# Sliding-window attention and a cosine-gated MLP on one core: where four matmuls of tile 0 stand, and how batch 0's shifted rows of v are made

## The chip, the core and the metric

One core of a Trainium2 chip runs the whole program. Its engines work side by side, each through its own list of instructions in order: TensorE (PE in the profile; PEld is its weight load), VectorE (DVE), ScalarE (ACT), GpSimd (POOL) and SyncE (SP). They wait for one another by semaphores. Transfers run on 16 DMA engines that all queues share: q0 is filled by GpSimd, q1 by SyncE. TensorE writes to PSUM, of which this kernel names eight banks: O0, O1, S, X0, X1 and three called t.

The metric is the device time in microseconds, the median of several executions. Before the change it is 306.59 us (306.25 to 306.64 in three runs).

## The reference

```python
# q, k, v: (8 batches, 8 heads, 576 rows, 64); w_in: (512, 2048); w_out: (2048, 512)
scores = scale * q @ k^T                      # scale = 1 / sqrt(64)
mask = (rel >= 0) & (rel < 64)                # rel = row of q - row of k
attn = exp(scores - max) / (sum + 1e-9)
x = (attn @ v)                                # (4608, 512): a row for each token, heads side by side
h = x @ w_in
out = (h * cos(h)) @ w_out                    # float32
```

## The kernel before

The 4608 rows are cut into nine tiles of 512 (MT); a batch has 576 rows, so a tile takes its rows from one or two batches. Rows are handled in blocks of 64: block j of a batch sees only the columns of blocks j - 1 and j. Two heads make a pair, and there are four pairs; `xT[mt]` holds a tile's x transposed, 128 rows of a pair by 512 columns.

For attention the names are: `tq`, `tk` (transpose q and k of a pair), `pq`, `pk` (copy them out of PSUM), `s` (scores of four blocks), `m` (negated maximum), `e` (exponential, ScalarE), `i` (reciprocal of the sum, VectorE), `n` (product with it, on GpSimd with `.p` or VectorE with `.d`), `w` (transpose the weights), `c` (copy that out of PSUM), `v` (weights times v, into `o_ps`) and `x` (copy `o_ps` into `xT`, on ScalarE with `.a` or VectorE with `.d`). The first number behind a name is the pair, the second the half of its blocks.

For the MLP, tile by tile: `first(mt, ff, ks, ...)` (line 348) is one matmul of 128 x 512: slice `ff` of h (16 of them) gets the part of pair `ks`. Four of them finish a slice; ScalarE takes its sine (cos as a shifted sine, line 513), VectorE multiplies (line 516), and 64 matmuls of line 528 make the tile's output.

Tile 0 and batch 0 have no work of an earlier tile to lie beside. Their order is written out by hand as a list of steps, FIRST (line 41), that one loop walks (line 482); it fixes the order on all engines. After it a planner (`at`, `pump`) puts the work of later batches between the slices of the current tile, by due times counted in slices.

In tile 0 the first three slices of h (SKEW = 3) start early: the step `h.p` does the matmuls of slices 0 to 2 for pair p as soon as x of that pair is there. Slices 3 to 15 follow, four matmuls each, once x is complete. Each slice takes the bank that H_FIRST lists: O1, X0, X1, S, O0, and again. The same banks have held the scores (S_FIRST).

The weights are multiplied with v in windows of 128 rows. An even window starts at a multiple of 128 and is loaded straight into slot 0, 2, 4 or 6 of `vtiles` (`load_v`, by GpSimd's DMAs). An odd slot is shifted by 64 rows and put together within SBUF: its partitions 0 to 63 are the even slot behind it, its partitions 64 to 127 the even slot ahead of it (`spread_v`, line 166). For batch 0 the step `z.1.p` is GpSimd's copy of the upper halves of slots 1, 3, 5 and 7, and `z.0.d` VectorE's copy of the lower halves of 1, 3 and 5. Batch 1's are made by two DMAs of SyncE, later ones by VectorE.

`l` in FIRST issues the next of the large loads, on GpSimd's queue: three parts of w_in, q and k of batch 1, two halves of w_out. `tb` loads ScalarE's sine table.

Of the kernel before, what the change touches and what calls it, by code (L numbers as in the profile page):

```python
# [10 lines left out]
def _safe_warn(msg, *a, **kw):  # L11
# [20 lines left out]
PAIRS = 4  # L32
# [3 lines left out]
SKEW = 3  # L36
# [4 lines left out]
FIRST = (  # L41
# [6 lines left out]
)  # L48


# [1 line left out]
def kernel(  # L52
# [9 lines left out]
    nc = tc.nc  # L62
# [18 lines left out]
    vtiles = [const.tile([128, NU - 1, d_model], BF16, name=f"v{i}") for i in range(3)]  # L81
# [21 lines left out]
    def bank(which, name):  # L103
        if which == "t":
            return ps_t.tile([128, 512], F32, tag="t", name=name)
        return ps.tile([128, 512], F32, tag=which, name=name)

    def copy(engine, out, in_):
        {"a": nc.scalar.copy, "p": nc.gpsimd.tensor_copy}.get(engine, nc.vector.tensor_copy)(out, in_)  # L109
# [46 lines left out]
    def values_of(b):  # L156
        return rowtiles[0][:, 0:8 * d_model].rearrange("p (s x) -> p s x", s=8) if b == B - 1 else vtiles[b % 3]

    def load_v(b, c):
        n = 128 if c < 4 else 64  # L160
        vt = values_of(b)[:n, 2 * c if c < 4 else 2 * c - 1]
        nc.gpsimd.dma_start(out=vt.rearrange("p (h d) -> p h d", h=H),  # L162
                            in_=v[b, :, c * 128:c * 128 + n, :].rearrange("h p d -> p h d"))


    def spread_v(b, half, engine="p"):
        vt = values_of(b)
        to, of = ((vt[0:64, 1:7:2], vt[0:64, 2:8:2]), (vt[64:128, 1:8:2], vt[64:128, 0:7:2]))[half]
        if engine == "dma":
            nc.sync.dma_start(out=to, in_=of)  # L170
        else:
            copy(engine, to, of)
# [18 lines left out]
    def put(name, b, p, engine=None):  # L191
        of = st.pop(("t" + name, b, p)).rearrange("d (c p) -> d p c", c=RC)
        to = halves(turned(b))[name][:, p].rearrange("d (p c) -> d p c", c=RC)
        if b or name == "k":
            copy(engine, to, of)
        elif engine == "a":
            nc.scalar.mul(to, of, scale)
        else:
            nc.vector.tensor_scalar(to, of, scale, None, ALU.mult)
# [33 lines left out]
    def g_scores(n, which):  # L233
        s_ps = bank(S_FIRST[which], "s_ps")
        units = groups[n]
        s_ps = s_ps[:, 0:len(units) * 128].rearrange("p (u c) -> p u c", c=128)
        m0 = 2 if units[0][2] else 0
        nc.tensor.matmul(out=s_ps.rearrange("p u c -> p (u c)"), lhsT=ident,
                         rhs=mask16[:, m0:m0 + len(units)].rearrange("p u c -> p (u c)"),
                         start=True, stop=False, skip_group_check=True)  # L240
        for u, (b, p, j) in enumerate(units):
            for h in range(2):
                d = slice(64 * h, 64 * h + 64)
                nc.tensor.matmul(out=s_ps[d, u].rearrange("p (a t) -> p a t", a=2), lhsT=q_cols(b, p, j)[d],
                                 rhs=k_cols(b, p, j)[d], start=False, stop=u == len(units) - 1, skip_group_check=True)
        st["s", n] = s_ps
        st.update({("cross", unit): 0 for unit in units})
# [100 lines left out]
    def first(mt, ff, ks, start, stop):  # L348
        if start:
            st["h", ff] = bank((H_FIRST, H_SECOND, H_BANKS)[min(mt, 2)][ff], "h_ps")  # L350
        nc.tensor.matmul(out=st["h", ff], lhsT=w_in_sb[:, ks, ff * 128:ff * 128 + 128],  # L351
                         rhs=st["xT", mt][:, ks], start=start, stop=stop)

    def skew(mt):
        return 5 if mt == 1 else SKEW

    def skewed(mt, ks, n):
        for ff in range(skew(mt)):
            first(mt, ff, ks, n == 0, n == PAIRS - 1)

    def last_rows(gT, o_sb):
# [19 lines left out]
    def pump(time):  # L381
        plan.sort(key=lambda x: x[:2])
        while plan and plan[0][0] <= time:
            _, _, fn, args = plan.pop(0)
            fn(*args)
# [3 lines left out]
    n = n_first  # L389
# [71 lines left out]
            load_heads(name, 0, p0, n)  # L461
    for c in range(4):
        load_v(0, c)
    loads = iter([(load_w_in, 0, 512), (load_w_in, 512, 1280), (load_w_in, 1280, 2048),
                  (load_heads, "q", 1), (load_heads, "k", 1), (load_w_out, 0, 8), (load_w_out, 8, 16)])

    def load():
# [3 lines left out]
    turn_s, turn_h = iter(range(100)), iter(range(100))  # L471
    steps = {"tq": lambda p: transposed("q", 0, (p,)), "tk": lambda p: transposed("k", 0, (p,)),
             "pq": lambda p, engine=None: put("q", 0, p, engine),
             "pk": lambda p, engine="a": put("k", 0, p, engine),
             "mk": put_masks, "l": load, "tb": sine_table, "h": lambda p: skewed(0, p, next(turn_h)),
             "z": lambda half, engine=None: spread_v(0, half, engine),
             "s": lambda p, g: g_scores(2 * p + g, next(turn_s) % 5), "m": lambda p, g: g_max(2 * p + g),
             "e": lambda p, g: g_exp(2 * p + g), "i": lambda p, g: g_inv(2 * p + g),
             "n": lambda p, g, engine: g_norm(2 * p + g, engine), "w": lambda p, g: g_trans(2 * p + g),
# [9 lines left out]
    for mt in range(n_mt):  # L489
        base = mt * T  # L490
        gT = []
        if mt:
            for ks in range(PAIRS):
                pump(max([base - 1] + [time for time, _, fn, args in plan
                                       if fn is put_x and args[:2] == (mt, ks)
                                       or mt == 1 and fn is values and args == (mt, ks + 1)]))
                if mt > 1 or ks < 2:
                    skewed(mt, ks, ks)
            if mt == 1:
                for ff in range(skew(1)):  # L500
                    for ks in range(2, PAIRS):
                        first(1, ff, ks, False, ks == PAIRS - 1)
        for ff in range(n_ff):
            for ks in range(PAIRS):
                if ff >= skew(mt):
                    first(mt, ff, ks, ks == 0, ks == PAIRS - 1)
            h_ps = st.pop(("h", ff))
            sin = moe.tile([128, MT], F32, tag="sin", name="sin", bufs=4)
            if ff % 2 == 0:
                gt = moe.tile([128, 2, MT], BF16, tag="gT", name="gT", bufs=n_ff // 2 + 2)  # L510
                gT.append(gt)
            e = ff % 2
            nc.scalar.activation(sin, h_ps, AF.Sin, bias=math.pi / 2.0)  # L513
            if ff == n_ff - 1 and mt < B - 1:
                exp_table()
            nc.vector.tensor_tensor(out=gt[:, e], in0=h_ps, in1=sin, op=ALU.mult)  # L516
            pump(base + ff)
        half = n_ff // 2 if mt == 0 else n_ff
        for ms0 in range(0, MT // 128, 2):
            o_sb = moe.tile([128, 2, d_model], F32, tag="out", name="out_sb", bufs=3)  # L520
            o_ps = [bank(which, "out_ps") for which in (("O0",) if mt == n_mt - 1 and ms0 else ("O0", "O1"))]
            for step, (lo, e) in enumerate([(lo, e) for lo in range(0, n_ff, half) for e in range(2)]):
                ms = ms0 + e
                if mt == n_mt - 1 and ms == MT // 128 - 1:
                    last_rows(gT, o_sb)
                    break
                for ff in range(lo, lo + half):
                    nc.tensor.matmul(out=o_ps[e], lhsT=gT[ff // 2][:, ff % 2, ms * 128:ms * 128 + 128],  # L528
                                     rhs=w_out_sb[:, ff], start=ff == 0, stop=ff == n_ff - 1)
                    if ff % 4 == 3:  # L530
                        if ff == n_ff - 1:
                            if mt or not ms0 or e:
                                copy("a" if e else "d", o_sb[:, e], o_ps[e])
                            else:
                                at(Q + 13.97, copy, "d", o_sb[:, e], o_ps[e])
                            if mt == n_mt - 1:
                                store(o_sb, mt, ms0, e, 1)
                        pump(base + Q + 4 * ms0 + step * half // 4 + ff % half // 4)
            if mt < n_mt - 1:
                at(base + T + (1.5 if mt else 3) + ms0 / 2, store, o_sb, mt, ms0, 0, 2)  # L540
# [30 lines left out]
```

## Time and profile before

| | |
|---|---|
| median of three runs | 306.59 us |
| profiled execution | 306.21 us |
| its span, first to last instruction | 304.3 us |
| TensorE busy (PE) | 291.6 us, 96% |
| ScalarE busy | 235.8 us, 77% |
| VectorE busy | 218.5 us, 72% |
| GpSimd busy | 171.1 us, 56% |
| granted TensorE clock | 1.00 in all stages |
| h's matmuls (L351) | 576, 127.3 us busy |
| output's matmuls (L528) | 560, 125.1 us busy |

Instructions are shown as engine, line, operation and output<-input. A row of a timeline has the start and the duration in us, the number of instructions merged (x3), and in brackets how long the engine was idle before and what ended that. "Busy" overstates TensorE a little, since its matmuls are pipelined and their ends modelled. Lines such as L109 are those of a helper that many steps call, so such a row is told by the names of its tiles. An engine's idle time costs something only where others wait for that engine.

### The profile page before, as it was taken

What the parts mean: (1) busy time and instruction counts of PE and PEld (TensorE: products, weight loads), DVE (VectorE), ACT (ScalarE), POOL (GpSimd) and SP (SyncE); (2) the same over time, 40 slices, a digit from 0 to 9 for tenths busy, and PEclk for the clock granted to TensorE, in tenths of its full rate; (3) what the DMA queues carried; (4) which work ended last, traced back from release to release, by engine and by line L of the source; (5) the groups of instructions that cost most, each with busy time, mean ns of one, the idle gap of its engine ahead of it and who ended that gap; (6) DMA issues with size and microseconds to landing.
All of it is one profiled execution on the core that took longest, in us unless ns stands there. A gap on an engine that the chain in (4) does not pass through costs nothing.

```text
span 304.3 us, 7887 instructions
## 1 busy us (share of the span) xinstructions
PE 291.6 (96%) x2668; PEld 141.7 (47%) x2668; DVE 218.5 (72%) x833; ACT 235.8 (77%) x787; POOL 171.1 (56%) x198
## 2 busy tenths in 40 slices
PE   2968999999999999999999999999999999999996
PEld 1744444544454445444544444444444454454443
DVE  2896889688787878787877787778788877236701
ACT  4798699967997799779987998799869986106600
POOL 8996156967774976497659765967533630000000
PEclk9999999999999999999999999999999999999999
DMA  8999999699979998999999999999993441011012
GB/s 155 175 211 207 208 159 136 100 162 178 230 132 153 220 165 138 148 196 190 143 159 204 185 121 173 151 220 126 185 171 107 87 132 61 0 72 70 0 69 71
DMA packets 165577, 43.88 MB, mean 144 GB/s; under 512 B 154720, under 2 KB 160800, under 8 KB 165536
## 3 DMA queue, kind: packets, MB, share of 16 engines
q0 software_dynamic: 99344, 18.06, 75.6%
q1 hardware_dynamic: 66048, 25.11, 40.7%
q8 instruction: 21, 0.34, 0.4%
q10 hardware_dynamic: 144, 0.20, 0.2%
q14 instruction: 20, 0.16, 0.2%
HBM read 36.70 MB, written 9.44 MB: 152 GB/s over the span
## 4 chain that ended last, share of the span: by engine, by line
PE 87%; ACT 6%; DVE 3%; DMA 1%; issue 1%; POOL 0%; SPq 0%; DVEq 0%; POOLq 0%; ACTq 0%
PE h_ps L351 41%; PE out_ps L528 37%; ACT e L288 4%; PE o_ps L330 3%; PE s_ps L261 3%; PE out_ps L366 1%; DMA first_f<-in_k_dram 1%; DVE s L277 1%; PE tq_ps L186 1%; ACT wT L109 0%; DVE w L302 0%; PE tk_ps L186 0%; DVE out_sb L109 0%; ACT L343 0%; ACT L346 0%
## 5 line engine op out<-in xcount | busy, mean ns | idle before, releaser
L351 PE MATMUL h_ps<-xT,w_in 128*128 128x512 bf16 x576 | 127.3, 379 | 1.3 <-DVE xT L109 0.6
L528 PE MATMUL out_ps<-w_out,gT 128*128 128x512 bf16 x560 | 125.1, 380 | 0.2 <-DVE gT L516 0.2
L516 DVE TENSOR_TENSOR gT<-h_ps,sin 128x512 bf16<-128x512 f32 x144 | 95.5, 689 | 35.4 <-ACT sin L513 35.1
L513 ACT ACTIVATE sin<-h_ps 128x512 f32<-128x512 f32 x144 | 83.0, 599 | 34.0 <-PE h_ps L351 32.8
L288 ACT ACTIVATE e<-s,negm 128x128 f32<-128x128 f32 x256 | 98.6, 387 | 0.3 <-DVE negm L277 0.3
L302 POOL TENSOR_TENSOR w<-e,rden 128x512 bf16<-128x512 f32 (+1 forms) x76 | 74.3, 992 | 31.7 <-DVE rden L295 28.9
L351 PEld LDWEIGHTS <-w_in 128*128 128x128 bf16 x576 | 55.8, 98 | 66.8 <-issue 1.8
L528 PEld LDWEIGHTS <-gT 128*128 128x128 bf16 x560 | 53.1, 98 | 62.5 <-issue 0.2
L277 DVE CUSTOM_DVE_ANT_0 s<-s_ps,mask 128x128 f32<-128x128 f32 x256 | 58.1, 285 | 0.1
L288 ACT ACTIVATION_READ_ACCUMULATOR e<-s,negm 128x1 f32 x256 | 47.9, 187 | 0.0
L149 POOL DMA_DIRECT2D rows<-in_q_dram x30 | 25.4, 865 | 26.8 <-DMA T<-rows 17.4
L162 POOL DMA_DIRECT2D v<-in_v_dram x35 | 29.8, 869 | 9.9 <-DMA rows<-in_k_dram 6.3
L109 ACT COPY out_sb<-out_ps 128x512 f32<-128x512 f32 (+1 forms) x18 | 10.1, 562 | 24.2 <-PE out_ps L528 18.7
L295 DVE RECIPROCAL rden<-den 128x4 f32<-128x4 f32 (+1 forms) x80 | 13.8, 172 | 19.5 <-ACT e L288 17.9
L149 POOL DMA_DIRECT2D rows<-in_k_dram x30 | 25.5, 896 | 1.8 <-DMA T<-rows 1.8
L277 DVE DVE_READ_ACCUMULATOR2_ANT negm<- 128x1 f32 x256 | 21.3, 83 | 0.0
L109 DVE CAST xT<-o_ps 128x512 bf16<-128x512 f32 x26 | 16.9, 680 | 6.1 <-PE o_ps L330 5.9
L109 DVE COPY out_sb<-out_ps 128x512 f32<-128x512 f32 x18 | 12.4, 689 | 12.0 <-PE out_ps L528 12.0
L288 ACT ACTIVATE e<-s_ps,negm 128x128 f32<-128x128 f32 x32 | 11.5, 448 | 1.4 <-DVE negm L273 1.4
L261 PE MATMUL s_ps<-T 64*64 64x128 bf16 x512 | 12.1, 221 | 0.0
L261 PEld LDWEIGHTS <-T 64*64 64x64 bf16 x512 | 8.2, 106 | 8.3 <-DVE negm L277 4.4
L330 PEld LDWEIGHTS <-v 128*64 128x64 bf16 x504 | 9.4, 112 | 4.2 <-issue 2.1
(56 smaller groups left out, 147.8 us busy)
## 6 DMA issues: line engine op xcount, KB each, us to landing
out_dram<-out_sb SPq DMA_DIRECT2D x16, 512.0 KB, 6.3
v<-in_v_dram POOLq DMA_DIRECT2D x28, 128.0 KB, 8.5
rows<-in_q_dram POOLq DMA_DIRECT2D x24, 128.0 KB, 5.2
rows<-in_k_dram POOLq DMA_DIRECT2D x24, 128.0 KB, 8.0
w_out<-in_moe_w_out_dram POOLq DMA_DIRECT2D x2, 1024.0 KB, 15.8
w_in<-in_moe_w_in_dram POOLq DMA_DIRECT2D x2, 768.0 KB, 11.6
wT<-w SPq DMA_TRANSPOSE x66, 3.9
out_dram<-out_sb SPq DMA_DIRECT2D x3, 256.0 KB, 2.0
```

The source lines that it names most:

```text
L109: {"a": nc.scalar.copy, "p": nc.gpsimd.tensor_copy}.get(engine, nc.vector.tensor_copy)(out, in_)
L149: nc.gpsimd.dma_start(out=rows(b)[lo:lo + n, slot * 512:slot * 512 + 512].rearrange("p (h d) -> p h d", h=H), in_={"q": q, "k": k}[name][b ...
L162: nc.gpsimd.dma_start(out=vt.rearrange("p (h d) -> p h d", h=H), in_=v[b, :, c * 128:c * 128 + n, :].rearrange("h p d -> p h d"))
L261: nc.tensor.matmul(out=s_ps[cross][to, u].rearrange("p (a t) -> p a t", a=2), lhsT=q_cols(b, p, j)[d], rhs=k_cols(b, p, j)[d], start=True, ...
L277: nc.vector.tensor_tensor_reduce(out=s[:, u], in0=s_ps[:, u], in1=mask[:, 2 - j % 2 if j else 0], scale=-scale if b else -1.0, scalar=BIG, ...
L288: nc.scalar.activation(e[:, u], s[:, u], AF.Exp, bias=negm[:, u:u + 1], scale=1.0 if n < n_first else -1.0, accum_out=den[:, u:u + 1])
L302: (nc.gpsimd if engine == "p" else nc.vector).tensor_tensor(out=w[:, 0:u], in0=e[:, 0:u], op=ALU.mult, in1=rden[:, 0:u].unsqueeze(2).to_br ...
L330: nc.tensor.matmul(out=o_ps[64 * h:64 * h + 64, 64 * i:64 * i + 64], lhsT=values_of(b)[:, max(j - 1, 0), 128 * p + 64 * h:128 * p + 64 * h ...
L351: nc.tensor.matmul(out=st["h", ff], lhsT=w_in_sb[:, ks, ff * 128:ff * 128 + 128], rhs=st["xT", mt][:, ks], start=start, stop=stop)
L513: nc.scalar.activation(sin, h_ps, AF.Sin, bias=math.pi / 2.0)
L516: nc.vector.tensor_tensor(out=gt[:, e], in0=h_ps, in1=sin, op=ALU.mult)
L528: nc.tensor.matmul(out=o_ps[e], lhsT=gT[ff // 2][:, ff % 2, ms * 128:ms * 128 + 128], rhs=w_out_sb[:, ff], start=ff == 0, stop=ff == n_ff - 1)
```

## The change

Two edits in the part before the planner, and what follows from them.

First, slices 3 and 4 of tile 0 also start early. A new step `hx.ff` does the matmuls of slice `ff` for pairs 0 and 1: `hx.3` behind `h.1`, `hx.4` behind `x.3`. The steps `h.2` and `h.3` become one, `hl`, which goes slice by slice through 0 to 4 and does pairs 2 and 3 of each (`last_pairs`, taken from what tile 1 had). The copy `x.3` goes from ScalarE to VectorE.

Second, batch 0's odd slots of v. GpSimd's step `z.1.p` is dropped. SyncE gets four DMAs at the start, which copy within SBUF, in this order: the lower half of slot 1, the upper halves of slots 1 and 3, the lower half of slot 3, the upper halves of slots 5 and 7. VectorE's step `z` copies only the lower half of slot 5.

```diff
-    "l i.0.0 e.1.1 pq.3.d i.1.0 m.2.0 pk.3.a e.2.0 n.0.0.p n.1.0.d z.1.p w.0.0 i.1.1 m.2.1 e.2.1 "
-    "s.3.0 s.3.1 c.0.1.d n.1.1.p c.0.0.d w.1.0 m.3.0 i.2.0 z.0.d c.1.0.a n.2.0.p w.1.1 c.1.1.d v.0 "
-    "i.2.1 v.1 n.2.1.p m.3.1 e.3.0 e.3.1 l x.0.d w.2.0 i.3.0 x.1.d h.0 c.2.0.a n.3.0.p w.2.1 h.1 "
-    "i.3.1 n.3.1.d w.3.0 c.2.1.a w.3.1 tb v.2 c.3.0.d x.2.a c.3.1.d v.3 l x.3.a h.2 h.3 "
+    "l i.0.0 e.1.1 pq.3.d i.1.0 m.2.0 pk.3.a e.2.0 n.0.0.p n.1.0.d w.0.0 i.1.1 m.2.1 e.2.1 "
+    "s.3.0 s.3.1 c.0.1.d n.1.1.p c.0.0.d w.1.0 m.3.0 i.2.0 z c.1.0.a n.2.0.p w.1.1 c.1.1.d v.0 "
+    "i.2.1 v.1 n.2.1.p m.3.1 e.3.0 e.3.1 l x.0.d w.2.0 i.3.0 x.1.d h.0 c.2.0.a n.3.0.p w.2.1 h.1 hx.3 "
+    "i.3.1 n.3.1.d w.3.0 c.2.1.a w.3.1 tb v.2 c.3.0.d x.2.a c.3.1.d v.3 l x.3.d hx.4 hl "
...
     def skew(mt):
-        return 5 if mt == 1 else SKEW
+        return 5 if mt < 2 else SKEW
+
+    def last_pairs(mt):
+        for ff in range(skew(mt)):
+            for ks in range(2, PAIRS):
+                first(mt, ff, ks, False, ks == PAIRS - 1)
 
     def skewed(mt, ks, n):
-        for ff in range(skew(mt)):
+        for ff in range(skew(mt) if mt else SKEW):
             first(mt, ff, ks, n == 0, n == PAIRS - 1)
...
     for c in range(4):
         load_v(0, c)
+    for lo, hi, of in ((0, 64, (1, 2)), (64, 128, (1, 4)), (0, 64, (3, 4)), (64, 128, (5, 8))):
+        to = slice(of[0], of[1], 2)
+        source = slice(of[0] + 1, of[1] + 1, 2) if lo == 0 else slice(of[0] - 1, of[1] - 1, 2)
+        nc.sync.dma_start(out=vtiles[0][lo:hi, to], in_=vtiles[0][lo:hi, source])
...
-             "mk": put_masks, "l": load, "tb": sine_table, "h": lambda p: skewed(0, p, next(turn_h)),
-             "z": lambda half, engine=None: spread_v(0, half, engine),
+             "mk": put_masks, "l": load, "tb": sine_table, "h": lambda p: skewed(0, p, next(turn_h)), "hl": lambda: last_pairs(0),
+             "hx": lambda ff: [first(0, ff, ks, ks == 0, False) for ks in range(2)],
+             "z": lambda: nc.vector.tensor_copy(vtiles[0][0:64, 5], vtiles[0][0:64, 6]),
...
             if mt == 1:
-                for ff in range(skew(1)):
-                    for ks in range(2, PAIRS):
-                        first(1, ff, ks, False, ks == PAIRS - 1)
+                last_pairs(mt)
```

What stands in a row on TensorE behind `h.1`, before the change: the last two of its three matmuls, each with its weight load, and then the transposition `w.3.0` (`tw_ps`). Names carry buffer numbers here.

```order
L351 LDWEIGHTS w_in_77
L351 MATMUL h_ps_526<-xT_514,w_in_77 128x512
L351 LDWEIGHTS w_in_77
L351 MATMUL h_ps_528<-xT_514,w_in_77 128x512
L311 LDWEIGHTS w_532
L311 MATMUL tw_ps_546<-ident_79,w_532 128x128
```

And with the change, where `h_ps_545` is slice 3:

```order
L351 LDWEIGHTS w_in_77
L351 MATMUL h_ps_529<-xT_517,w_in_77 128x512
L351 LDWEIGHTS w_in_77
L351 MATMUL h_ps_531<-xT_517,w_in_77 128x512
L351 LDWEIGHTS w_in_77
L351 MATMUL h_ps_545<-xT_517,w_in_77 128x512
L351 LDWEIGHTS w_in_77
L351 MATMUL h_ps_545<-xT_517,w_in_77 128x512
L311 LDWEIGHTS w_535
L311 MATMUL tw_ps_552<-ident_79,w_535 128x128
```

Two matmuls of slice 3 have come ahead of `w.3.0`.

On TensorE again, behind `v.3` (L330), before the change: pair 2 of slices 0, 1 and 2, then pair 3.

```order
L330 LDWEIGHTS v0_74
L330 MATMUL o_ps_581<-wT_579,v0_74 64x64
L351 LDWEIGHTS w_in_77
L351 MATMUL h_ps_524<-xT_514,w_in_77 128x512
L351 LDWEIGHTS w_in_77
L351 MATMUL h_ps_526<-xT_514,w_in_77 128x512
L351 LDWEIGHTS w_in_77
L351 MATMUL h_ps_528<-xT_514,w_in_77 128x512
L351 LDWEIGHTS w_in_77
L351 MATMUL h_ps_524<-xT_514,w_in_77 128x512
```

And with the change, where `h_ps_606` is slice 4 and `h_ps_527` slice 0:

```order
L330 LDWEIGHTS v0_74
L330 MATMUL o_ps_587<-wT_585,v0_74 64x64
L351 LDWEIGHTS w_in_77
L351 MATMUL h_ps_606<-xT_517,w_in_77 128x512
L351 LDWEIGHTS w_in_77
L351 MATMUL h_ps_606<-xT_517,w_in_77 128x512
L351 LDWEIGHTS w_in_77
L351 MATMUL h_ps_527<-xT_517,w_in_77 128x512
L351 LDWEIGHTS w_in_77
L351 MATMUL h_ps_527<-xT_517,w_in_77 128x512
```

The two matmuls of slice 4 that need only pairs 0 and 1 stand ahead of the first that needs pair 2, and slice 0 is finished by the two that follow.

On GpSimd, from the load of batch 1's k on, the difference is that its copy for v (L109) is gone and four products `n` (L302) stand together (a minus marks rows of before, a plus those of the change):

```order
 L142 DMA rows_73<-in_q_dram 128x4x576
 L142 DMA rows_73<-in_k_dram 128x4x576
-L302 TENSOR_TENSOR w<-e,rden 128x512
-L109 COPY v_74<-v_74 64x4x512
-L302 TENSOR_TENSOR w<-e,rden 128x512 x3
+L302 TENSOR_TENSOR w<-e,rden 128x512 x4
 L178 DMA w_out<-in_moe_w_out_dram 128x8x512
 L302 TENSOR_TENSOR w<-e,rden 128x512
```

The product `n.1.1` now follows `n.0.0` directly.

## The prediction

> **What bounds the kernel now.** I read the page's busy shares first, then the stages by windows, then the chain of waits, then the timelines of single engines from 15 to 31 us. The windows cut the span where the chain changes hands:
>
> ```profile
> core 0: us, PE busy (x) PEld busy (x) DVE busy (x) ACT busy (x) POOL busy (x), PEclk, DMA share, GB/s
> 11.40:25.20 13.80, 10.60 (x209) 6.92 (x206) 11.62 (x25) 13.77 (x65) 13.64 (x14) 1.00 1.32 204
> 25.20:304.30 279.10, 275.45 (x2350) 130.74 (x2349) 202.09 (x795) 216.19 (x708) 147.16 (x165) 1.00 1.17 141
> ```
>
> From 11.4 to 25.2 us ScalarE has no free time (13.77 of 13.80 us) while TensorE waits 3.2 us. After 25.2 us TensorE works 275.45 of 279.10 us. So TensorE's list of matmuls sets the end from there on: a matmul taken out of that stretch shortens the span by its own time, as long as nothing else becomes late. The chain of waits shows the hand-over (start, duration, what):
>
> ```profile
> 23.19 1.28 ACT L346
> ...
> 24.68 0.48 ACT xT L109
> ```
>
> The sine table's load, behind exponentials and copies without a pause, and then the copy of x's pair 2 lie on ScalarE. The copy ends at 25.16 us, and TensorE's dense stretch starts behind it. The change shortens none of these steps, so I leave its start at 25.21 us. TensorE around it (start, duration; in brackets what it waited):
>
> ```profile
> 19.06 0.90 PE L330 MATMUL o_ps<-wT,v 128*64 128x64 bf16 x32
> ...
> 20.91 0.81 PE L351 MATMUL h_ps<-xT,w_in 128*128 128x512 bf16 x3 [0.59 <-DVE xT L109]
> ...
> 22.89 0.40 PE L311 MATMUL tw_ps<-ident,w 128*128 128x128 bf16 x4 [0.30 <-POOL w L302]
> 23.45 0.40 PE L311 MATMUL tw_ps<-ident,w 128*128 128x128 bf16 x4 [0.16 <-DVE w L302]
> 23.77 0.90 PE L330 MATMUL o_ps<-wT,v 128*64 128x64 bf16 x32
> 25.21 5.77 PE L351 MATMUL h_ps<-xT,w_in 128*128 128x512 bf16 x26 [0.53 <-ACT xT L109]
> 30.91 0.28 PE L186 MATMUL tq_ps<-ident,rows 64*64 64x64 bf16 x10
> ```
>
> Ahead of 25.21 us stand h.0 and h.1, three matmuls each; the other 58 of tile 0's 64 lie behind.
>
> **The four matmuls.** 26 of them fill 25.21 to 30.91 us: 0.219 us each. The change puts two (hx.3) behind h.1, where TensorE waits 0.30 and then 0.16 us, and two (hx.4) behind v.3, where it waits 0.53 us. Two take 0.44 us: they fit the last wait, and the first two waits together (0.46 us). So 54 instead of 58 are left at 25.21 us: 4 x 0.219 = 0.88 us gained.
>
> What has to be there for it: hx.3 and hx.4 use xT of pairs 0 and 1 only, and banks S and O0, whose scores ScalarE has read before it loads the sine table. Pair 3's copy moves from ScalarE to VectorE, which has nothing else then; v.3 ends at 23.77 + 0.90 = 24.67 us, and a copy of this size takes 0.68 us (below, 20.18 us), so it ends near 25.4 us. Slice 0's matmul with pair 2 runs from 25.21 to 25.43 us, the one with pair 3 behind it without a wait. Were it later, the gain would shrink by the lateness.
>
> Behind them slice 5 needs bank O1 back, for which VectorE's product of slice 0 must be done:
>
> ```profile
> 26.90 3.71 DVE L516 TENSOR_TENSOR gT<-h_ps,sin 128x512 bf16<-128x512 f32 x6 [2.59 <-ACT sin L513]
> ```
>
> Six products take 3.71 us, so the first ends by 27.6 us. Slice 0 is now complete after 2 dense matmuls instead of 4, so that becomes 27.15 us; slice 5 starts at 25.21 + 10 x 0.219 = 27.4 us. No cost, with 0.25 us to spare.
>
> **POOL and VectorE.** The copies that spread v:
>
> ```profile
> 15.23 2.33 POOL L109 COPY v<-v 64x2048 bf16<-64x2048 bf16 x1
> 17.64 3.21 POOL L302 TENSOR_TENSOR w<-e,rden 128x512 bf16<-128x512 f32 x3
> ```
>
> ```profile
> 15.73 0.17 DVE L295 RECIPROCAL rden<-den 128x4 f32<-128x4 f32 x1
> ...
> 17.73 1.49 DVE L109 COPY v<-v 64x1536 bf16<-64x1536 bf16 x1
> ...
> 20.18 0.68 DVE L109 CAST xT<-o_ps 128x512 bf16<-128x512 f32 x1
> ```
>
> POOL's 2.33 us go: n.1.1 needs the reciprocal of 15.73 us, so it ends near 15.9 + 3.21 / 3 = 17.0 instead of 18.7 us. VectorE's 1.49 us become one slot of three, 0.5 us. w.1.1 and v.0 could run from 17.9 instead of 19.06 us. At 25.21 us this alone moves nothing, because ScalarE isn't waiting; it gives v.0 room for what comes now.
>
> **The four DMAs.** They copy 64, 128, 64 and 128 KB inside SBUF and wait for v's chunks. First the last chunk's issue; then, from the DMA issues, its landing, that of the spread of batch 1's v, and that of the last stores (KB, us to landing):
>
> ```profile
> 8.07 0.93 POOL L162 DMA_DIRECT2D v<-in_v_dram  x1
> ```
>
> ```profile
> v<-in_v_dram POOLq DMA_DIRECT2D x1, 128.0 KB, 6.0
> v<-v SPq DMA_DIRECT2D x1, 256.0 KB, 6.1
> out_dram<-out_sb SPq DMA_DIRECT2D x3, 256.0 KB, 2.0
> ```
>
> The last chunk lands at 14.1 us, so the fourth DMA is issued near 14.2 us. The stores, with the DMA engines to themselves, bound its landing by 16.2 us, the spread beside a full q0 by 20.3 us. The engines are full here too, but the DMAs are smaller and issued over 2 us; I take 18 us. When would it hurt? Behind v.0 TensorE has v.1, v.2, v.3 (0.45 us each, half of an L330 row), four w (0.40 each), h.0 and h.1 (0.66 each) and four single matmuls (0.88): 5.15 us. Counted back from 25.21 us, v.0 must end by 20.1 us and the DMAs must land by about 20.0 us. Cost: 0 at 18 us, 0.3 us at the upper bound. On SyncE nothing stands behind them but batch 1's spread, which waits for loads from 23.7 us on.
>
> **q0 is delayed.** The DMAs take time from POOL's loads. What batch 1's spread took shows the price; the first row is 42 to 46 us, the others 46 to 50 us (packets, MB, share):
>
> ```profile
> q0 software_dynamic: 4858, 0.61, 240.2%
> ```
>
> ```profile
> q0 software_dynamic: 2972, 0.37, 146.6%
> q1 hardware_dynamic: 480, 0.46, 43.4%
> ```
>
> q0 lost 0.24 MB in 4 us, 1.6 us at its undisturbed rate. The new DMAs move 0.39 of 0.46 MB: 1.35 us, between 0.9 (if a third overlaps) and 1.6 us. All loads behind land that much later, w_out's second half among them, for which POOL waits:
>
> ```profile
> 22.76 0.94 POOL L178 DMA_DIRECT2D w_out<-in_moe_w_out_dram  x1
> ...
> 41.11 3.32 POOL L149 DMA_DIRECT2D rows<-in_q_dram  x4 [4.50 <-PE s_ps L261]
> ...
> 48.92 0.82 POOL L302 TENSOR_TENSOR w<-e,rden 128x384 bf16<-128x384 f32 x1 [2.05 <-PE s_ps L261]
> ```
>
> ```profile
> w_out<-in_moe_w_out_dram POOLq DMA_DIRECT2D x1, 1024.0 KB, 17.3
> ```
>
> It lands at 22.76 + 17.3 = 40.1 us. The releaser named at 41.11 us is doubtful: this load also waits for w_out's semaphore. Behind these loads stands the softmax product of 48.92 us, and TensorE transposes it as soon as it ends. POOL has 2.05 us of room there, of which 0.88 go because TensorE's side comes earlier: 1.17 us are left for a delay of 1.35. Cost: 0.1 us, with bounds 0 and 0.4 (a delay of 1.6). Batch 1's rows have more room:
>
> ```profile
> 30.22 0.69 POOL L162 DMA_DIRECT2D v<-in_v_dram  x1 [1.94 <-DMA rows<-in_k_dram]
> ```
>
> ```profile
> 33.15 0.22 PE L186 MATMUL tk_ps<-ident,rows 64*64 64x64 bf16 x2
> ```
>
> k's rows are in by 30.22 us and are read at 33.15 us: 2.9 us, against 0.88 + 1.35.
>
> **Sum.** The profiled execution has a span of 304.3 us and took 306.21 us. -0.88 + 0 + 0.1 = -0.78, that is 305.4 us for it; on the median of 306.59 us: 305.8 us.
>
> **Rivals.** A: the landing and q0's delay eat more. Both at their upper ends cost 0.3 + 0.4 instead of 0.1 us: up to 306.4 us; I take 306.2. For it: 1.35 stands close to 1.17 us. Against it: POOL's next products wait for VectorE and let it catch up. 18 in 100.
>
> B, slower: the DMAs of v stay behind w_in's large packets. First 16 to 20 us on q0, then w_in's second part:
>
> ```profile
> q0 software_dynamic: 562, 0.84, 115.3%
> ```
>
> ```profile
> w_in<-in_moe_w_in_dram POOLq DMA_DIRECT2D x1, 768.0 KB, 10.7
> ```
>
> ```profile
> 9.68 0.82 POOL L175 DMA_DIRECT2D w_in<-in_moe_w_in_dram  x1
> ```
>
> 562 packets in 4 us are 8.8 per us and DMA engine, 0.114 us each, against 0.013 us from 42 to 46 us. If an engine sends a long run of them between two of the DMAs, these land behind w_in's second part (9.68 + 10.7 = 20.4 us), at 21.4: 1.4 us late, 306.59 - 0.88 + 1.4 = 307.1 us. Behind the third part, as large and so 3.7 us later (0.84 MB in 4 us), they land at 25.1: 310.8 us. As its time I take the middle, 309. It decides from 20.9 us on, where the 0.88 us are gone. For it: no row has such a DMA beside such packets. Against it: SyncE's stores from 76 to 78.6 us, which had nearly all of the engines while loads waited:
>
> ```profile
> q1 hardware_dynamic: 504, 0.93, 94.7%
> q0 software_dynamic: 315, 0.04, 23.2%
> ```
>
> 15 in 100.
>
> The Trainium skill, "DMA: Bandwidth & Descriptors", Queues, rings and completion order, speaks for B: a DMA engine changes from one ring to another only after a whole packet, typically 9 to 17 descriptors. An estimate from that page: 17 of the above rows' packets, taken as descriptors, are 1.9 us, four turns 7.8 us, a landing near 22.5 us and 308.2 us in all. The stores from 76 to 78.6 us do not agree with turns as even as that.
>
> C: the gain is there and given back. Batch 2's second transposition by DMA, its landing, and the scores that read it:
>
> ```profile
> 65.09 4.58 SPq L153 DMA_TRANSPOSE T<-rows  x1
> ```
>
> ```profile
> T<-rows SPq DMA_TRANSPOSE x1, 8.3
> ```
>
> ```profile
> 73.61 0.64 PE L261 MATMUL s_ps<-T 64*64 64x128 bf16 x32
> ```
>
> It lands at 73.4 us, 0.2 us ahead of them. If its start does not move up with TensorE, 0.2 of 0.88 us are left: 306.4 us. Against it: its loads are issued behind softmax products that do move. 8 in 100.
>
> **How the numbers follow.** The forecast has 59 in 100, with a range of its own from 305.4 (no cost, and 0.3 us from small waits) to 306.1 us. What a measurement of this kernel can tell from no change is 0.2%, 0.6 us, so faster is below 305.98 us. The forecast gives 54 of faster and 5 of same, A 4 and 14, C 0 and 8, B 1 of same and 14 of slower: 0.58, 0.28 and 0.14. The range takes in A, C and B's near end: 305.3 to 307.0 us.
>
> **What would show it.** Right: four L351 matmuls more ahead of 25.2 us, in two pairs; no wait of 0.53 us; the first transposition for batch 1 at 30.0 instead of 30.91 us; later waits of TensorE as before. DMAs: v.0, the first L330, starts by 18.5 and ends by 20.1 us. q0: POOL's loads start near 42.5 instead of 41.11 us, and the transposition near 49 us waits under 0.3 us more for POOL. Wrong: a wait for v beyond 20.1 us (B), a dense stretch that starts after 25.4 us, or a new wait of TensorE near 73 us (C).

## The result, and the profile after

| | before | after |
|---|---|---|
| median of the runs | 306.55 us (306.14 to 307.55, 6 runs) | 309.25 us (308.74 to 309.86, 6 runs) |
| ratio | | 1.0079, 95% interval 1.006 to 1.0098 |
| profiled execution / its span | 306.21 / 304.3 us | 309.43 / 307.4 us |

The change made the kernel slower by 2.70 us, where 0.8 us faster was forecast. The same windows as before, cut where the profile after changes its character:

```profile
core 0: us, PE busy (x) PEld busy (x) DVE busy (x) ACT busy (x) POOL busy (x), PEclk, DMA share, GB/s
11.40:19.00 7.60, 6.96 (x148) 4.66 (x143) 6.89 (x16) 7.28 (x39) 5.39 (x6) 1.00 1.46 207
19.00:23.00 4.00, 1.91 (x43) 1.36 (x41) 2.35 (x9) 4.00 (x24) 2.97 (x3) 1.00 1.17 227
23.00:26.50 3.50, 3.50 (x12) 1.48 (x12) 1.41 (x3) 2.97 (x8) 3.45 (x4) 0.51 1.17 206
26.50:304.00 277.50, 276.56 (x2387) 131.78 (x2386) 203.22 (x797) 216.57 (x710) 147.04 (x165) 1.00 1.18 141
```

Two stretches are new. From 19 to 23 us TensorE does 1.91 us of work in 4 us. From 23 to 26.5 us it is busy without a pause, but at a granted clock of 0.51: twelve matmuls take 3.5 us. The dense stretch behind that is as before. TensorE's timeline says what it waited for, and how slow the matmuls then are:

```profile
19.25 0.25 PE L330 MATMUL o_ps<-wT,v 128*64 128x64 bf16 x4
19.74 0.25 PE L330 MATMUL o_ps<-wT,v 128*64 128x64 bf16 x4 [0.24 <-DMA v<-v]
20.48 0.25 PE L330 MATMUL o_ps<-wT,v 128*64 128x64 bf16 x4 [0.49 <-DMA v<-v]
21.89 0.51 PE L330 MATMUL o_ps<-wT,v 128*64 128x64 bf16 x20 [1.16 <-DMA v<-v]
...
22.93 1.32 PE L351 MATMUL h_ps<-xT,w_in 128*128 128x512 bf16 x3 [0.20 <-DVE xT L109]
24.05 0.63 PE L311 MATMUL tw_ps<-ident,w 128*128 128x128 bf16 x4
24.47 2.24 PE L351 MATMUL h_ps<-xT,w_in 128*128 128x512 bf16 x5
26.55 0.61 PE L311 MATMUL tw_ps<-ident,w 128*128 128x128 bf16 x8
27.09 1.01 PE L330 MATMUL o_ps<-wT,v 128*64 128x64 bf16 x32
28.04 4.25 PE L351 MATMUL h_ps<-xT,w_in 128*128 128x512 bf16 x18
```

v.0 waits three times for the new DMAs, 1.89 us in all. The four rows of 32 matmuls are v.0 and v.1 together; they end at 22.4 us instead of 20.0 us. Five matmuls of h.1 and hx.3 then take 2.24 us; at the full clock the same five take 1.24 us (e3 below). The chain of waits (start, duration) goes through the fourth DMA, where before it went through ScalarE:

```profile
6.42 6.11 DMA v<-in_v_dram
14.47 7.29 DMA v<-v
22.93 1.32 PE h_ps L351 x3
```

The fourth DMA is issued at 14.47 us and lands at 21.76 us. None of the four moved a packet before 16.4 us, 3.9 us after the first was issued. From 16 to 20 us the queues moved (packets, MB, share):

```profile
q0 software_dynamic: 425, 0.63, 86.4%
q1 hardware_dynamic: 344, 0.30, 28.9%
```

Of q0's 562 packets before, 425 are left; so SyncE's small packets pass beside w_in's, but in 4 us only 0.30 of their 0.39 MB. ScalarE, which set the start of the dense stretch before, now waits for TensorE:

```profile
24.71 0.59 ACT L109 COPY wT<-tw_ps 128x512 bf16<-128x512 bf16 x1 [0.51 <-PE tw_ps L311]
25.32 1.28 ACT L346 ACT_TABLE_LOAD   x1
...
27.58 0.59 ACT L109 CAST xT<-o_ps 128x512 bf16<-128x512 f32 x1 [0.76 <-PE o_ps L330]
```

The sine table is loaded 2.1 us later than before (23.19 us), x.2's copy comes 2.9 us later (24.68 us). Comparing instruction by instruction, the sines lag 2.60 us from 30 us on and 2.88 us from 122 us on.

This profiled execution also began 1.5 us late, because the first load of k landed later. By 18.7 us, where w.1.1 starts, it was level with the kernel before. The late start is no part of the change: the profile of e2 below has the waits for the DMAs without it.

### The profile page after: what moved, and what is told of

The parts are those of the page before. It is cut to its first block, busy times and chain, and to the rows that moved or that the text cites. A ratio compares the mean times of both kernels' runs of the same rounds, so it can differ in the third digit from the quotient of the medians.

```text
span 307.4 us, 7894 instructions
## 1 busy us (share of the span) xinstructions
PE 293.5 (95%) x2668; PEld 142.5 (46%) x2668; DVE 217.9 (71%) x834; ACT 235.5 (77%) x786; POOL 168.6 (55%) x197
## 4 chain that ended last, share of the span: by engine, by line
PE 81%; DMA 5%; POOL 4%; DVE 3%; ACT 2%; issue 2%; SPq 1%; POOLq 0%; DVEq 0%
PE h_ps L351 41%; PE out_ps L536 32%; PE o_ps L330 3%; PE s_ps L261 3%; DMA v<-v 2%; DMA v<-in_v_dram 2%; POOL w L302 2%; DVE s L277 1%; PE out_ps L371 1%; DMA wT<-w 1%; POOL rows L142 1%; ACT e L288 1%; ACT L343 1%; PE tw_ps L311 1%; SPq L472 1%
## 5 line engine op out<-in xcount | busy, mean ns | idle before, releaser
L351 PE MATMUL h_ps<-xT,w_in 128*128 128x512 bf16 x576 | 129.0, 382 | 0.4 <-DVE xT L109 0.2
L302 POOL TENSOR_TENSOR w<-e,rden 128x512 bf16<-128x512 f32 (+1 forms) x76 | 74.1, 989 | 33.4 <-DVE rden L295 30.5
L109 ACT COPY out_sb<-out_ps 128x512 f32<-128x512 f32 (+1 forms) x18 | 10.2, 566 | 24.2 <-PE out_ps L536 18.7
L109 DVE CAST xT<-o_ps 128x512 bf16<-128x512 f32 x27 | 17.6, 681 | 7.6 <-PE o_ps L330 7.2
L109 DVE COPY out_sb<-out_ps 128x512 f32<-128x512 f32 x18 | 12.4, 689 | 12.0 <-PE out_ps L536 12.0
L330 PE MATMUL o_ps<-wT,v 128*64 128x64 bf16 x504 | 11.7, 197 | 2.1 <-DMA v<-v 1.9
L330 PEld LDWEIGHTS <-v 128*64 128x64 bf16 x504 | 9.7, 112 | 6.6 <-issue 2.7
```

Source lines behind the costliest of these rows:

```text
L302: (nc.gpsimd if engine == "p" else nc.vector).tensor_tensor(out=w[:, 0:u], in0=e[:, 0:u], op=ALU.mult, in1=rden[:, 0:u].unsqueeze(2).to_br ...
L330: nc.tensor.matmul(out=o_ps[64 * h:64 * h + 64, 64 * i:64 * i + 64], lhsT=values_of(b)[:, max(j - 1, 0), 128 * p + 64 * h:128 * p + 64 * h ...
```

## The experiments

One number is needed to read them. Each run gives its mean granted clock. Of 83 runs of the kernel before, on three chips, 25 had 1.00 (median 306.38 us); 49 had 0.994, which is one stretch of 3.4 us at half clock (306.71 us); nine had 0.989, two such stretches (308.44 us). The profile on which the prediction rests has 1.00. The six runs after the change had 0.987 to 0.994.

When a slow stretch comes can be read from the clock records of the twelve profiles. The clock changes only at the edges of a grid with cells of 3.41 us, and the grid lies elsewhere in each execution. Once the clock had first risen, seven cells up to 30 us were followed by one at half clock: TensorE had worked 1.15 to 2.05 us in them. In every cell that the full clock followed it had worked 2.02 us or more. So the border lies near 2.0 of 3.41 us. Here are four cells (start:end, length, then TensorE's work), of the profile before (full clock follows), of after and e1 (half clock follows) and of e5 (full clock follows):

```profile
15.13:18.55 3.42, 2.02 (x26) 1.20 (x26) 3.42 (x9) 3.42 (x20) 3.28 (x3) 1.00 1.17 211
19.66:23.08 3.42, 1.49 (x33) 1.11 (x34) 1.77 (x6) 3.42 (x21) 2.68 (x4) 1.00 1.15 223
16.02:19.43 3.41, 2.05 (x35) 1.32 (x37) 3.41 (x7) 3.41 (x20) 3.33 (x3) 1.00 1.16 211
15.22:18.63 3.41, 3.06 (x31) 1.56 (x31) 3.41 (x8) 3.41 (x19) 3.18 (x3) 1.00 1.18 211
```

The profile before only just kept its clock. With a grid 2.4 us later its cell from 17.50 to 20.91 us would have held 1.66 us of work. That 58 of the 83 runs have a slow stretch fits this; none of those runs was profiled, so where it lies in them is not shown.

**e1: the four matmuls alone.** The edits of h, with v's copies as before.

```diff
-    for lo, hi, of in ((0, 64, (1, 2)), (64, 128, (1, 4)), (0, 64, (3, 4)), (64, 128, (5, 8))):
...
-             "z": lambda: nc.vector.tensor_copy(vtiles[0][0:64, 5], vtiles[0][0:64, 6]),
+             "z": lambda half, engine=None: spread_v(0, half, engine),
```

> The matmuls alone: hx.3, hx.4, hl and pair 3's copy on VectorE as in the change, batch 0's shifted rows of v by the copies of GpSimd and VectorE as before. My theory (the matmuls gain 0.88 us and all the loss comes from v's DMAs): 305.7 us, 0.88 us under before, clock 1.00, the dense stretch of L351 from 25.2 us with four fewer matmuls in it. Rival (the early slices themselves cost time, through a bank or through the copy of pair 3): 306.6 us or more, with a wait of TensorE at the first dense matmul of slice 0 or at slice 5.

Measured: 306.82 us (12 runs) against 306.81 us; ratio 0.9999, 0.9976 to 1.0022. No gain where 0.88 us was expected. Eleven of the twelve runs had a clock of 0.994 or less. Its profile, TensorE's timeline and two windows:

```profile
18.78 0.40 PE L311 MATMUL tw_ps<-ident,w 128*128 128x128 bf16 x4 [1.19 <-POOL w L302]
...
25.52 5.32 PE L351 MATMUL h_ps<-xT,w_in 128*128 128x512 bf16 x23 [0.16 <-issue]
```

```profile
19.40:22.90 3.50, 3.10 (x39) 2.13 (x41) 2.82 (x8) 3.35 (x19) 3.48 (x5) 0.51 1.16 212
22.90:304.00 281.10, 274.61 (x2357) 132.25 (x2391) 203.96 (x799) 218.18 (x711) 149.74 (x167) 1.00 1.15 141
```

After 1.19 us of waiting for w.1.1's product the clock is halved from 19.4 us on. The first transposition for batch 1 starts at 30.76 us, only 0.15 us earlier than before. Before the change TensorE could lose that time in its later waits of 0.59, 0.30, 0.16 and 0.53 us; now the four matmuls fill those waits. That is an argument from two profiles; e5 and e6 test it.

**e2: the DMAs alone.** The edits of v with h's order of before.

```diff
+    for lo, hi, of in ((0, 64, (1, 2)), (64, 128, (1, 4)), (0, 64, (3, 4)), (64, 128, (5, 8))):
...
+             "z": lambda: nc.vector.tensor_copy(vtiles[0][0:64, 5], vtiles[0][0:64, 6]),
```

> v's DMAs alone: four DMAs of SyncE and one copy of VectorE, the order of h's matmuls as before. My theory: the last DMA lands near 21 us, v.0 ends after it, TensorE's clock falls below 1.00 behind that wait, and the time is that of the change plus 0.9 us, 310 us. Rival (the loss comes from the two parts together): under 308 us.

Measured: 309.62 us (6 runs), ratio 1.0077, 1.0048 to 1.0106. This half alone brings the whole loss:

```profile
20.16 0.32 PE L330 MATMUL o_ps<-wT,v 128*64 128x64 bf16 x4 [2.11 <-DMA v<-v]
20.91 0.32 PE L330 MATMUL o_ps<-wT,v 128*64 128x64 bf16 x4 [0.43 <-DMA v<-v]
22.38 0.75 PE L330 MATMUL o_ps<-wT,v 128*64 128x64 bf16 x20 [1.15 <-DMA v<-v]
```

```profile
19.50:26.30 6.80, 4.34 (x41) 2.78 (x43) 2.70 (x6) 4.24 (x19) 4.42 (x6) 0.50 1.17 220
```

Waits of 3.69 us, and here two stretches of half clock, 19.5 to 26.3 us. The time is 0.37 us above that of the change, where 0.9 us was expected; the two were not run beside one another.

**e3: the change, with eight matmuls inside v.0 whose result nothing reads,** so that TensorE has work while it waits for the DMAs.

```diff
+            if (mt, p) == (0, 0):
+                for _ in range({1: 1, 3: 2, 5: 5}.get(i, 0)):
+                    nc.tensor.matmul(out=filler, lhsT=ident, rhs=mask16[:, 0:4].rearrange("p u c -> p (u c)"),
+                                     start=True, stop=True, skip_group_check=True)
```

> The change with eight matmuls of 128 x 512 on nobody's account inside v.0 (one ahead of slot 1, two ahead of slot 3, five ahead of slot 5), 1.75 us of work in the 1.9 us in which TensorE waits for v's DMAs. Theory 'clock' (the wait makes the granted clock fall to 0.54 from 22.9 us on, and that costs 1 to 1.5 us beyond the wait itself): the clock stays at 1.00 and the time falls by 1 to 1.5 us against the change, to about 308 us. Rival 'wait alone' (the clock costs nothing, since ScalarE is late anyway): the same as the change, 309.2 us, or slower by what of the eight matmuls does not fit.

Measured: 309.26 us (10 runs), ratio 1.0076, 1.0043 to 1.0109, as the change itself. But only half of the runs held the full clock: those five have a median of 308.25 us (307.95 to 309.24), the five others took 309.27 to 313.20 us. The profiled run is one of the first five:

```profile
19.05 0.25 PE L331 MATMUL o_ps<-wT,v 128*64 128x64 bf16 x4 [0.63 <-DMA v<-v]
...
22.20 0.51 PE L331 MATMUL o_ps<-wT,v 128*64 128x64 bf16 x20 [0.99 <-DMA v<-v]
...
24.11 1.24 PE L356 MATMUL h_ps<-xT,w_in 128*128 128x512 bf16 x5
25.18 0.61 PE L311 MATMUL tw_ps<-ident,w 128*128 128x128 bf16 x8
```

v.0 and v.1 end 0.3 us later than after the change, yet the eight transpositions start at 25.18 instead of 26.55 us. So the halved clock is worth about 1.4 us in these two profiles, and 309.25 - 308.25 = 1.0 us in the medians, where the second is one of five runs picked by their clock.

**e4: the DMAs, read by nobody.** e1 with the four DMAs added; they write to batch 2's odd slots, which are overwritten later, and v's copies are as before.

```diff
+    for lo, hi, of in ((0, 64, (1, 2)), (64, 128, (1, 4)), (0, 64, (3, 4)), (64, 128, (5, 8))):
...
+        nc.sync.dma_start(out=vtiles[2][lo:hi, to], in_=vtiles[0][lo:hi, source])
```

> The matmuls alone as in the first of these runs, and the four DMAs besides, into the odd slots of batch 2's v, which nobody reads before they are written again. It shows what the DMAs cost by delaying q0 and nothing else. My forecast's term: 0.1 us over the matmuls alone (0 to 0.4), w_out's second half 1.35 us later (0.9 to 1.6). Rival (the delay of q0 is what costs the 2.7 us): 308 us or more, with a wait of TensorE for GpSimd's product near 49 us or for batch 1's rows near 30 us.

Measured: 307.12 us (12 runs), ratio 1.0011, 0.9984 to 1.0038: 0.30 us above e1, under the rival's 308 us. Its profiled run had the full clock, and there the sines are 0.87 us ahead of before from 30 us on: the four matmuls' gain, as forecast. Then it is lost in two places:

```profile
49.61 0.34 PE L311 MATMUL tw_ps<-ident,w 128*128 128x128 bf16 x3 [0.77 <-POOL w L302]
```

```profile
121.70 0.47 PE L330 MATMUL o_ps<-wT,v 128*64 128x64 bf16 x18 [0.76 <-DMA wT<-w]
```

```profile
42.93 3.32 POOL L149 DMA_DIRECT2D rows<-in_q_dram  x4 [4.69 <-DMA v<-in_v_dram]
...
48.66 1.67 POOL L302 TENSOR_TENSOR w<-e,rden 128x384 bf16<-128x384 f32 x2
```

The second half of w_out lands at 41.89 us (before 40.07), so POOL's loads start at 42.93 instead of 41.11 us; the product behind them has no wait any more (2.05 us before), and its transposition waits 0.77 us. Not all of this is the DMAs': without them these loads start at 42.44 us in e1 and at 42.55 us in e11.

**e5 and e6: TensorE kept busy without the DMAs.** Seven matmuls that nothing reads, five ahead of w.1.1 and two ahead of h.0, in e1 (e5) and in the kernel before (e6).

```diff
-    "s.3.0 s.3.1 c.0.1.d n.1.1.p c.0.0.d w.1.0 m.3.0 i.2.0 z.0.d c.1.0.a n.2.0.p w.1.1 c.1.1.d v.0 "
+    "s.3.0 s.3.1 c.0.1.d n.1.1.p c.0.0.d w.1.0 m.3.0 i.2.0 z.0.d c.1.0.a n.2.0.p f.5 w.1.1 c.1.1.d v.0 "
...
+    def fill(n, which):
+        filler = bank(which, "filler")
+        for _ in range(n):
+            nc.tensor.matmul(out=filler, lhsT=ident, rhs=mask16[:, 0:4].rearrange("p u c -> p (u c)"),
+                             start=True, stop=True, skip_group_check=True)
```

> The matmuls alone (no DMAs of v), with seven matmuls on nobody's account in TensorE's waits: five ahead of w.1.1, where it waits 1.2 us for GpSimd, two ahead of h.0. Theory 'clock hides the gain' (with the early slices TensorE has no room left between 19 and 25 us, and when the granted clock is halved there for 3.4 us, as in that run's profile, the 0.88 us are lost again): the clock stays at 1.00 and the median is 305.7 us, 0.9 us under before on the same chip. Rival (the early slices gain nothing in themselves): as before, 306.6 to 306.8 us, at a clock of 1.00.

> The kernel before with the same seven matmuls in the same waits, the control for the run above. Theory 'clock hides the gain': before has room for a halved clock in its waits, so its median falls by 0.2 to 0.4 us only, to 306.4 us, and the run above is 0.7 us under this one. Rival: the two runs have the same time.

Measured: e5 305.81 us (12 runs), ratio 0.9976, 0.995 to 1.0001; e6 306.55 us (12 runs), ratio 0.9995, 0.9976 to 1.0014; before 306.59 us. All 24 runs had the full clock. So the filler alone gives nothing (0.2 to 0.4 us was expected), and with it the four matmuls give 306.55 - 305.81 = 0.74 us. e5's interval just takes in 1, so it was run again (e11). In e5's profile:

```profile
17.38 1.24 PE L479 MATMUL filler<-mask,ident 128*128 128x512 bf16 x5
18.70 0.40 PE L311 MATMUL tw_ps<-ident,w 128*128 128x128 bf16 x4
...
24.79 5.31 PE L351 MATMUL h_ps<-xT,w_in 128*128 128x512 bf16 x23 [0.16 <-issue]
30.04 0.48 PE L186 MATMUL tq_ps<-ident,rows 64*64 64x64 bf16 x36
```

The time ahead of w.1.1 is filled, w.1.1 itself starts as before, and the first transposition for batch 1 starts at 30.04 us, where 30.0 was forecast.

**e7: the change, with the large loads behind the DMAs.** The second and third part of w_in and batch 1's q and k are issued near 17.7 us.

```diff
-    "tk.2 s.1.1 i.0.1 tq.3 l m.0.0 m.1.0 pk.2.d n.0.1.p s.2.0 l w.0.1 tk.3 s.2.1 e.0.0 l e.1.0 m.1.1 "
-    "l i.0.0 e.1.1 pq.3.d i.1.0 m.2.0 pk.3.a e.2.0 n.0.0.p n.1.0.d w.0.0 i.1.1 m.2.1 e.2.1 "
-    "s.3.0 s.3.1 c.0.1.d n.1.1.p c.0.0.d w.1.0 m.3.0 i.2.0 z c.1.0.a n.2.0.p w.1.1 c.1.1.d v.0 "
+    "tk.2 s.1.1 i.0.1 tq.3 m.0.0 m.1.0 pk.2.d n.0.1.p s.2.0 w.0.1 tk.3 s.2.1 e.0.0 e.1.0 m.1.1 "
+    "i.0.0 e.1.1 pq.3.d i.1.0 m.2.0 pk.3.a e.2.0 n.0.0.p n.1.0.d w.0.0 i.1.1 m.2.1 e.2.1 "
+    "s.3.0 s.3.1 c.0.1.d n.1.1.p l l l l c.0.0.d w.1.0 m.3.0 i.2.0 z c.1.0.a n.2.0.p w.1.1 c.1.1.d v.0 "
```

> The change with four of GpSimd's large loads (w_in's second and third part, batch 1's q and k) issued behind the product n.1.1, near 17 us, instead of from 9.7 to 14 us, so that v's DMAs have only w_in's first part beside them. Theory 'they wait for q0's packets': the last of the four lands by 18.5 us instead of 21.8 us, TensorE's waits inside v.0 shrink from 1.9 to under 0.3 us and the clock does not fall behind them; later loads are 2 to 3 us late, which costs up to 2 us near 30, 33 or 49 us, so the total may be anything from 306 to 308 us. Rival 'the DMAs are slow by themselves': they land 7 us after their issue here too.

Measured: 309.72 us (7 runs), ratio 1.0094, 1.0063 to 1.0124. The four DMAs, issued at 12.61 to 14.53 us as before, now land at 18.15, 18.34, 18.52 and 18.70 us, right behind w_in's first part (17.96 us). So they are not slow by themselves: they lie behind and beside q0's packets. TensorE no longer waits for v, but the 306 to 308 us that were expected are missed: it waits because POOL issues four loads ahead of n.2.0, the clock is halved from 21.65 to 25.06 us behind these waits, and later TensorE waits for what now lands late:

```profile
20.30 0.44 PE L330 MATMUL o_ps<-wT,v 128*64 128x64 bf16 x16 [1.21 <-ACT wT L109]
21.87 0.61 PE L311 MATMUL tw_ps<-ident,w 128*128 128x128 bf16 x4 [1.13 <-POOL w L302]
```

```profile
52.87 0.34 PE L311 MATMUL tw_ps<-ident,w 128*128 128x128 bf16 x3 [1.52 <-POOL w L302]
```

**e8: the kernel before with 28 small matmuls near its start,** to warm TensorE up early.

```diff
+    warm = bank("X1", "warm")
+    for _ in range(28):
+        nc.tensor.matmul(out=warm[:, 0:128], lhsT=ident, rhs=ident, start=True, stop=True, skip_group_check=True)
```

> The kernel before with 28 matmuls of 128 x 128 on nobody's account at the start, from 1.4 to about 4.4 us, when TensorE waits for the first rows. In the profile of before a 128x512 matmul takes 0.61 us up to 11.6 us and 0.39 us behind. Theory: the matmuls up to 11.6 us run at the lower clock because TensorE stood still before; with work at the start they run at 0.39 us by 6 us, the chain through TensorE from 7.0 to 10.7 us shortens by 1 to 1.5 us, and so does the total: 305.3 us. Rival: the early pace is set by something else, or ScalarE and the loads hold the chain at the same times: 306.6 us.

Measured: 307.79 us (12 runs), ratio 1.0034, 1.0012 to 1.0056: slower, where 305.3 us was expected. Windows of its profile:

```profile
4.90:8.30 3.40, 1.58 (x68) 1.29 (x64) 1.76 (x8) 1.55 (x4) 3.40 (x6) 1.00 1.09 155
8.30:11.70 3.40, 2.93 (x72) 2.40 (x67) 2.80 (x6) 2.73 (x12) 3.30 (x5) 0.50 2.01 163
```

The clock rises early, and falls again for a stretch behind a cell in which TensorE has only 1.58 us of work, and once more from 18.6 to 22.0 us. The table of the profile before gives 1.00 for the first 11.4 us too, but that is not the speed there: its clock records begin at 11.7 us, and a 128x512 matmul takes 0.61 us at 10.66 and 0.39 us at 12.05 us. Two of the runs had the full clock and took 307.65 and 307.79 us, so something else costs here too; it was not followed.

**e11 and e12: e5 once more, and e5 with e4's unread DMAs,** on one chip.

> The edits of h with the seven filler matmuls once more, beside the kernel before on the same chip, to narrow the interval. Theory (the four matmuls are worth 0.7 to 0.9 us as long as TensorE's clock is not halved): granted clock 1.00 in every run, median 0.7 to 0.9 us below the kernel before, ratio 0.997 to 0.998. Rival (the gain of the first such run was the chip's mood on that day): ratio 0.999 to 1.001, or runs at 0.994 among the others.

> The kernel of e5 with the four DMAs of SyncE added, whose copies go to batch 2's odd slots of v and are read by nobody; v's copies as before. What the DMAs' traffic alone costs, at full clock. Theory (q0 comes later by 1.6 us, POOL waits for w_out and the softmax product near 49 us is late): 0.5 to 0.8 us above e5 in that place and 0 to 0.8 us more near 122 us, so 306.3 to 307.3 us in all; the profile shows a wait of L311 for w of 0.5 to 0.8 us near 49.6 us. Rival (the DMAs cost only through who waits for them): 305.7 to 306.0 us as e5, no such wait. If the wait near 122 us belongs to the DMAs, it stands in this profile and not in the other one of this pair; if it comes by chance, it is as likely in either.

Measured, against 306.49 us: e11 305.71 us (305.33 to 306.56, 11 runs), ratio 0.9965, 0.9945 to 0.9985; e12 307.01 us (306.18 to 310.61, 12 runs), ratio 1.0019, 0.9991 to 1.0047. All runs at 0.998 or more. e11 confirms the gain, 0.78 us. The DMAs' traffic alone, waited for by nobody, costs 307.01 - 305.71 = 1.3 us, inside the 0.5 to 1.6 us that were expected. Only a part of it can be pointed at, because the two profiled executions are not typical: e11's is its slowest run (306.56 us), e12's is faster than its median (306.34 us). The transposition near 49 us, in the profiles of e11 and of e12:

```profile
49.22 0.34 PE L311 MATMUL tw_ps<-ident,w 128*128 128x128 bf16 x3 [0.32 <-POOL w L302]
```

```profile
49.44 0.34 PE L311 MATMUL tw_ps<-ident,w 128*128 128x128 bf16 x3 [0.60 <-POOL w L302]
```

e11 has some of that wait without the DMAs, since w_out landed at 41.51 us there (e5: 40.92, e12: 41.73). And the wait for wT that stood near 122 us in e4 is missing in e12, while e11 has one of its kind elsewhere:

```profile
89.81 1.01 PE L330 MATMUL o_ps<-wT,v 128*64 128x64 bf16 x52 [0.65 <-DMA wT<-w]
```

It isn't tied to the DMAs: e8 has one too (0.47 us at 121.49 us). How far the DMAs make such waits likelier is open.

**Where the 2.7 us lie.** Step by step from the kernel before: -0.78 us for the four matmuls (e11), +1.30 us for the traffic (e12 over e11), +1.24 us for v being late (e3's runs at full clock, 308.25, over e12), +1.00 us for the halved clock (the change over those). Each step starts where the one ahead of it ends, so they make 309.25 - 306.49 = 2.76 us whatever the runs between took: this divides the loss, it does not test it. The profiles, by the lag of the sines near the end, divide it a little otherwise: -0.85 us (e5), then +0.6 (e12), +1.9 (e3) and +1.2 us (the change). Traffic and lateness together are 2.5 us either way. How much of that is traffic alone stays open between 0.6 and 1.3 us.

## Why the prediction was wrong

- **The bound.** Right: behind the hand-over TensorE's list sets the end, and a matmul out of it is worth its own time.
- **The four matmuls, -0.88 us.** Right in mechanism and size: 0.87 us in the profiles of e4 and e5, 0.74 and 0.78 us in medians. It needed a condition that no step named: TensorE at the full clock. The profile showed 1.00 in all stages, and I took that for the kernel; in 58 of 83 runs it isn't so. The waits that I filled can absorb a slow stretch (e1: no gain; e5, where the clock stays up: the gain).
- **The copy of x.3 and bank O1's return, no cost.** Right: in e5 no wait stands between 25 and 30 us.
- **POOL and VectorE.** Right: v.0 starts at 17.8 us in e2, where I had 17.9, and then waits for the DMAs. VectorE's one slot was cheaper, 0.26 us after the change, where I took 0.5.

```profile
19.17 0.26 DVE L486 COPY v<-v 64x512 bf16<-64x512 bf16 x1
```

- **The landing of v's DMAs. The step that failed.** "I take 18 us", between bounds of 16.2 and 20.3 us; it was 21.76 us, and 22.2 us in e2. The upper bound was no bound: batch 1's spread shared its engines with packets of 0.013 us, these with packets of 0.114 us. The prediction had both numbers and used the second only for rival B. What the DMAs did in its place: no packet for 3.9 us, and then packets side by side with w_in's (344 beside 425 in 4 us), and a landing of the last 1.7 us ahead of w_in's second part (23.46 us). The limit of 20.0 us was about right: v is late by some 2 us, which costs 2.1 us in profiles (the sines at 30 us: 1.23 us behind in e3, 0.87 us ahead in e5) and 1.24 us in medians, by a median of e12 that takes in runs from 306.18 to 310.61 us.
- **The granted clock.** No term stood for it. A wait of TensorE was priced at its length; but cells with little work drop the clock, and the waits in v.0 cost 1.0 us more in medians, 1.2 to 1.4 us in profiles, through the half clock behind them. This is the second step that failed: a term that stood at nothing.
- **q0's delay, +0.1 us with bounds 0 and 0.4.** Right place. The delay itself, 1.35 us, was fair: w_in's third part lands at 25.81 to 26.63 us with the DMAs (e2, e4, e12) and at 24.26 to 25.10 us without (before, e1, e5, e11), w_out's second half at 41.73 and 41.89 us (e12, e4) for 40.07 to 41.51 us. What was wrong is the room of 1.17 us, read from one profile: POOL's wait there is 0.33 us in e5, and in e11 it is gone and TensorE waits 0.32 us, both without the DMAs. With them TensorE waits 0.77 us (e4) and 0.60 us (e12). After the change itself it does not wait there, because TensorE is later than POOL:

```profile
52.41 0.34 PE L311 MATMUL tw_ps<-ident,w 128*128 128x128 bf16 x3
```

- **The rivals.** B, at 15 in 100, is the nearest: w_in's packets hold the DMAs up, and they decide from 20.9 us on. But they landed ahead of w_in's second part, not behind it as B has it. Its 307.1 us for a landing at 21.4 us lacked the clock and the traffic; the 309 us taken for its middle came near by luck, since the DMAs did not wait for the third part either. The argument against it, the stores from 76 to 78.6 us, was about packets of another size (23.2% for 315 packets). Of A's two prices the first, 0.3 us, was far too low; the second, 0.4 us, cannot be told from the scatter of w_out's landing. C's wait near 73 us is not there after the change.

The Trainium skill, "DMA: Bandwidth & Descriptors", Queues, rings and completion order, lets a DMA engine change rings only after a packet of several descriptors; the estimate from it was a landing at 22.5 us and 308.2 us in all (its own terms, 14.2 + 7.8, make 22.0 us). The landing of 21.76 us agrees with that better than with my bound. How long the turns of a single DMA engine are is not shown: the 344 and 425 packets from 16 to 20 us are sums over all of them, and the 3.9 us without a packet stand in no term of the estimate. The Trainium skill, "TensorE: Matmul & The Clock Gate", Part 1, has the clock at 4/8 after an idle window of about 3.4 us. The traces agree with the half (0.51) and with the length of the slow stretch (3.4 us), but not with a whole idle window as the condition: the longest single wait ahead of it was 1.16 us after the change and 1.19 us in e1, and the cells of 3.41 us ahead held 1.49 and 2.05 us of work.

## What to carry to other kernels

Before filling a wait on TensorE, look at the granted clock of many runs, not of one profile: a wait may be the slack in which a slow stretch disappears (argued here, not traced in the kernel before), and then the gain comes only if TensorE is also kept busy ahead of it. Here seven matmuls that nothing reads, added to the four moved ones, took the time from that of the kernel before (e1) to 0.78 us below it (e11); without the DMAs, that version beats both kernels. Price a small DMA by the packets that lie on the engines at that moment, not by a copy of its size at another time, and count for every byte what is queued behind it, even when nobody waits for the copy itself.

## What the runs showed of the hardware

- Four copies of 64 to 128 KB inside SBUF took 5.6 to 7.3 us beside w_in's load (after the change; 5.2 to 8.2 us in e2 and e3), and 4.2 to 5.5 us when only w_in's first part was ahead of them (e7: issue 12.61 and 13.20, landing 18.15 and 18.34; 14.53 to 18.70 us).
- The half clock comes without any long pause. TensorE's clock changed only on a grid of 3.41 us: cells with 1.15 to 2.05 us of work were followed by a cell at half clock, also where TensorE worked all through that one (after the change, 23.1 to 26.5 us); cells with 2.02 us and more kept the full clock. The grid lies elsewhere in each execution, so one program has the slow stretch in some runs and not in others (kernel before: 58 of 83 with it).
- w_out's second half, issued at the same time within 0.13 us, landed between 40.07 and 41.51 us in six kernels without the DMAs (before, e1, e5, e6, e8, e11).
